# Linear attention's numerator with the sequence on the partitions: many short matmuls and transposes in place of few long ones

## The chip, the cores and the metric

The kernel runs on one core of one Trainium2 chip. A core has a matrix engine (TensorE, PE in the profile, with its weight loads listed apart as PEld), a vector engine (DVE), a scalar engine (ACT), GpSimd (POOL), and DMA queues that SyncE (SP) starts. Matmul results land in PSUM, in tiles of one bank each; this kernel's PSUM pool has 8 such tiles and every PSUM tile comes from it. DVE and ACT carry results from PSUM to SBUF. The kernel is written in a tile framework that works out the semaphores, gives out the buffers and may move an instruction against its neighbours.

The metric is the device time of one execution in microseconds, the median of several runs.

## The reference

Two linear attention blocks A and B with their own weights read the same input `x` (2048 rows, 640 columns, 32 heads of 20 columns). A gate mixes their outputs row by row.

```python
def _A_ref(x, wqkv, wo):                    # _B_ref is the same with B's weights
    H = 32; Dh = D // H                     # D = 640, Dh = 20, S = 2048
    q, k, v = ...(x @ wqkv)...              # each (B, H, S, Dh)
    phi = lambda t: jnp.where(t > 0, t + 1, jnp.exp(t)) + 1e-6
    pq, pk = phi(q), phi(k)
    kv = jnp.einsum("bhsd,bhse->bhde", pk, v)
    z = jnp.einsum("bhsd->bhd", pk)
    num = jnp.einsum("bhqd,bhde->bhqe", pq, kv)
    den = jnp.einsum("bhqd,bhd->bhq", pq, z)[..., None] + 1e-6
    o = num / den
    return o.transpose(...).reshape(B, S, D) @ wo

g = sigmoid((x * gate_w).sum(-1, keepdims=True))
out = g * A(x) + (1 - g) * B(x)
```

## The kernel before

The kernel keeps `x` transposed (`xT`, columns of `x` on the partitions, S = 2048 along the free side). In the constants, `P` is 128, `NCH` 512, `NS` = 4 blocks of 512 rows, `NQ` = 4 chunks of 128 rows in a block, `ST` = 16 chunks in all, and `DT` = `QT` = 5 tiles of 128 columns.

`q_group` makes 128 columns of phi(q) for 512 rows, transposed: 5 matmuls of 512 columns, two ACT activations, one DVE instruction that writes `pqT`. `kv_chunk` makes phi(k) and v for 128 rows with the rows on the partitions, in three PSUM tiles: 15 matmuls, two `ke` activations and two `vaug` copies on ACT, two `kr` instructions and one `pk` on DVE.

```python
def kv_chunk(blk, i, with_gate):
    # ... p0: 512 wide, p1: 448 wide, p2: 320 wide; 5 matmuls each
    nc.scalar.activation(out=e[:, 0:K0_W], in_=p0[:, 0:K0_W], func=ACT.Exp)          # ke
    nc.scalar.activation(out=e[:, K0_W:D], in_=p1[:, 0:K1_W], func=ACT.Exp)          # ke
    nc.vector.tensor_scalar(r[:, 0:K0_W], p0[:, 0:K0_W], 0.0, 1e-6, ...)             # kr
    nc.vector.tensor_scalar(r[:, K0_W:D], p1[:, 0:K1_W], 0.0, 1e-6, ...)             # kr
    nc.vector.scalar_tensor_tensor(out=pk[:, i, :], in0=e[:], in1=r[:], ...)         # pk
    nc.scalar.copy(out=vaug[...], in_=p1[...])      # first 16 heads of v
    nc.scalar.copy(out=vaug[...], in_=p2[...])      # last 16 heads of v
```

`phase_kvwin` then sums phi(k) times v over all rows. It leaves `KVbd`, a 640 by 640 matrix that holds the 20 by 20 block of each head on its diagonal and zeros elsewhere, and `Zsel`, with which `den_group` makes the 32 denominators of 128 rows, the rows on the partitions. `rec_ops` takes the reciprocals and multiplies them by the gate into `recs`, 32 values for each row.

The part that the change replaces is the numerator and its scaling. The result has to be `oT`, transposed, since `final_group` uses it as the stationary operand:

```python
def transposes(self, n):                       # of RecState
    pr = ps_tile_bf16(f"recT_{self.blk}")
    for q in range(NQ):
        i = n * NQ + q
        nc.tensor.transpose(out=pr[:H, q * P:(q + 1) * P], in_=self.recs[:, i, :], identity=identb[:])
    nc.vector.tensor_copy(out=self.recT[:H, n * NCH:(n + 1) * NCH], in_=pr[:H, :NCH])

def num_group(blk, oT, recT, j, n):
    dch = echunks[j]                           # the 2 or 3 tiles of pqT whose heads reach into tile j
    pn = ps_tile(f"num_{blk}")
    pr = ps_tile(f"rt_{blk}")
    for kk, c in enumerate(dch):
        nc.tensor.matmul(
            pn[:, :NCH], lhsT=KVbd[:, c, j * P:(j + 1) * P], rhs=pqT[:, c, n * NCH:(n + 1) * NCH],
            start=(kk == 0), stop=(kk == len(dch) - 1),
        )
    nc.tensor.matmul(                          # spreads 32 reciprocals over the 20 columns of each head
        pr[:, :NCH], lhsT=E[:, j * P:(j + 1) * P], rhs=recT[:, n * NCH:(n + 1) * NCH],
        start=True, stop=True,
    )
    numsb = work.tile([P, NCH], BF16, tag="numsb", name="numsb")
    nc.scalar.copy(out=numsb[:], in_=pn[:, :NCH])
    nc.vector.tensor_tensor(
        out=oT[:, j, n * NCH:(n + 1) * NCH], in0=numsb[:], in1=pr[:, :NCH], op=ALU.mult,
    )
```

`echunks` has 2, 3, 3, 3 and 2 tiles for the five values of j, 13 in all, so a block of the reference takes 4 x 13 = 52 `num` matmuls and 4 x 5 = 20 `rt` matmuls, each 512 columns wide, and 16 transposes of `recs`.

`final_group(i)` multiplies 128 rows of `oTA` and `oTB` by the two output matrices: 20 matmuls of 320 columns into two PSUM tiles, one copied out by ACT and one by DVE, then one DMA to the output.

The order in the program, from the denominators of A on:

```python
for i in range(LEAD_KV):                 # 4
    kv_chunk("B", i, False)
for n in range(NS):
    recA.transposes(n)
for n in range(NS):
    for j in range(QT):
        num_group("A", oTA, recTA, j, n)         # 20 groups in a row
# ... kv_chunk B 4 to 15, with q_group B of blocks 0 to 2 laid between them
phase_kvwin("B", ZselB)
# ... den_group B 0 to 11 and their rec_ops
for m in range(QT):
    q_group("B", m, NS - 1)
for n in range(NS - 1):
    recB.transposes(n)
# ... num_group B of block 0; den_group B 12 to 15 and their rec_ops
for n in range(NS):
    # ... for n > 0: num_group B of block n, 5 groups
    for q in range(NQ):
        final_group(n * NQ + q)
```

Of the kernel before, what the change touches and what calls it, by code (L numbers as in the profile page):

```python
# [8 lines left out]
P = 128  # L9
FP32 = mybir.dt.float32  # L10
BF16 = mybir.dt.bfloat16
ACT = mybir.ActivationFunctionType
ALU = mybir.AluOpType
# [3 lines left out]
def kernel(  # L17
# [11 lines left out]
    nc = tc.nc  # L29
# [3 lines left out]
    S, D = x2.shape  # L33
    H = 32
    Dh = D // H
    assert D % H == 0 and D % P == 0 and S % P == 0
    DT = D // P
    ST = S // P
    NCH = min(512, S)
    assert S % NCH == 0 and NCH % P == 0  # L40
    NS = S // NCH
    NQ = NCH // P
    QT = D // P
# [19 lines left out]
    for c in range(DT):  # L63
        h_lo = (c * P) // Dh
        h_hi = ((c + 1) * P - 1) // Dh
# [7 lines left out]
    echunks = []  # L73
# [7 lines left out]
    persist = ctx.enter_context(tc.tile_pool(name="persist", bufs=1))  # L81
    consts = ctx.enter_context(tc.tile_pool(name="consts", bufs=1))
    work = ctx.enter_context(tc.tile_pool(name="work", bufs=2))
    psum = ctx.enter_context(tc.tile_pool(name="psum", bufs=8, space=bass.MemoryType.PSUM))

    def ps_tile_bf16(name):
        return psum.tile([P, 2 * NCH], BF16, tag="ps", name=name)

    def ps_tile(name):
        return ps_tile_bf16(name).bitcast(FP32)  # L90
# [5 lines left out]
    pqT = persist.tile([P, QT, S], BF16, name="pqT")  # L96
    pk = persist.tile([P, ST, D], BF16, name="pk")
    vaug = persist.tile([P, ST, VAUG_W], BF16, name="vaug")
    oTA = persist.tile([P, QT, S], BF16, name="oTA")
    oTB = persist.tile([P, QT, S], BF16, name="oTB")  # L100
    KVbd = persist.tile([P, DT, D], BF16, name="KVbd")
    ZselA = persist.tile([P, DT, H], BF16, name="ZselA")
    ZselB = persist.tile([P, DT, H], BF16, name="ZselB")
    recTA = persist.tile([P, S], BF16, name="recTA")
    recTB = persist.tile([P, S], BF16, name="recTB")
    recsA = persist.tile([P, ST, H], BF16, name="recsA")
    recsB = persist.tile([P, ST, H], BF16, name="recsB")

    identb = consts.tile([P, P], BF16, name="identb")
    make_identity(nc, identb[:])  # L110
    E = consts.tile([P, D], BF16, name="E")
# [3 lines left out]
        out=E[:H], in_=E[:H], pattern=[[1, D]], compare_op=ALU.is_ge, fill=0.0, base=0,  # L115
# [3 lines left out]
        out=E[:H], in_=E[:H], pattern=[[-1, D]], compare_op=ALU.is_ge, fill=0.0, base=Dh - 1,  # L119
        channel_multiplier=Dh,  # L120
    )
    nc.vector.memset(recTA[:], 0.0)
    nc.vector.memset(recTB[:], 0.0)
    nc.gpsimd.memset(  # L124
        vaug[:].rearrange("p i (h t) -> p i h t", t=Dh + 1)[:, :, :, Dh:Dh + 1], 1.0
    )
# [4 lines left out]
    gcol = consts.tile([P, ST], FP32, name="gcol")  # L131
    gcolB = consts.tile([P, ST], FP32, name="gcolB")
# [72 lines left out]
    def kv_chunk(blk, i, with_gate: bool):  # L205
        nB = K1_W + V0_W
        nC = V1_W + (1 if with_gate else 0)
        sl = slice(i * P, (i + 1) * P)
        p0 = ps_tile(f"p0_{blk}")
        p1 = ps_tile(f"p1_{blk}")  # L210
        p2 = ps_tile(f"p2_{blk}")
        regions = [(p0, K0_W, OFF_K0), (p1, nB, OFF_K1), (p2, nC, OFF_V1)]
        for pt, w, off in regions:
            for c in range(DT):
                first, last = (c == 0), (c == DT - 1)
                nc.tensor.matmul(pt[:, :w], lhsT=xT[:, c, sl], rhs=Wr[:, c, off:off + w], start=first, stop=last)  # L216
        e = work.tile([P, D], BF16, tag="ke", name="ke")
        r = work.tile([P, D], BF16, tag="kr", name="kr")
        nc.scalar.activation(out=e[:, 0:K0_W], in_=p0[:, 0:K0_W], func=ACT.Exp)  # L219
        nc.scalar.activation(out=e[:, K0_W:D], in_=p1[:, 0:K1_W], func=ACT.Exp)  # L220
        nc.vector.tensor_scalar(r[:, 0:K0_W], p0[:, 0:K0_W], 0.0, 1e-6, op0=ALU.max, op1=ALU.add)
        nc.vector.tensor_scalar(r[:, K0_W:D], p1[:, 0:K1_W], 0.0, 1e-6, op0=ALU.max, op1=ALU.add)
        nc.vector.scalar_tensor_tensor(  # L223
            out=pk[:, i, :], in0=e[:], scalar=1.0, in1=r[:], op0=ALU.min, op1=ALU.add,
        )
        nc.scalar.copy(
            out=vaug[:, i, 0:VSPLIT_H * (Dh + 1)].rearrange("p (h t) -> p h t", t=Dh + 1)[:, :, 0:Dh],
            in_=p1[:, K1_W:K1_W + V0_W].rearrange("p (h t) -> p h t", t=Dh),
        )
        nc.scalar.copy(  # L230
            out=vaug[:, i, VSPLIT_H * (Dh + 1):VAUG_W].rearrange("p (h t) -> p h t", t=Dh + 1)[:, :, 0:Dh],
            in_=p2[:, 0:V1_W].rearrange("p (h t) -> p h t", t=Dh),
        )
        if with_gate:
            nc.scalar.activation(out=gexp[:, i:i + 1], in_=p2[:, nC - 1:nC], func=ACT.Exp, scale=-1.0)
# [31 lines left out]

    class RecState:

        def __init__(self, blk, Zsel, gc, recs, recT):  # L270
            self.blk = blk
            self.Zsel = Zsel
            self.gc = gc
            self.recs = recs
            self.recT = recT
            self.den_tiles = [ps_tile(f"den{n}_{blk}") for n in range(NS)]

        def den_group(self, i):
# [16 lines left out]
                op=ALU.mult,  # L295
            )

        def transposes(self, n):
            pr = ps_tile_bf16(f"recT_{self.blk}")
            for q in range(NQ):  # L300
                i = n * NQ + q
                nc.tensor.transpose(out=pr[:H, q * P:(q + 1) * P], in_=self.recs[:, i, :], identity=identb[:])
            nc.vector.tensor_copy(out=self.recT[:H, n * NCH:(n + 1) * NCH], in_=pr[:H, :NCH])

    def num_group(blk, oT, recT, j, n):
        dch = echunks[j]
        pn = ps_tile(f"num_{blk}")
        pr = ps_tile(f"rt_{blk}")
        for kk, c in enumerate(dch):
            nc.tensor.matmul(  # L310
                pn[:, :NCH], lhsT=KVbd[:, c, j * P:(j + 1) * P], rhs=pqT[:, c, n * NCH:(n + 1) * NCH],
                start=(kk == 0), stop=(kk == len(dch) - 1),
            )
        nc.tensor.matmul(  # L314
            pr[:, :NCH], lhsT=E[:, j * P:(j + 1) * P], rhs=recT[:, n * NCH:(n + 1) * NCH],
            start=True, stop=True,
        )
        numsb = work.tile([P, NCH], BF16, tag="numsb", name="numsb")
        nc.scalar.copy(out=numsb[:], in_=pn[:, :NCH])  # L319
        nc.vector.tensor_tensor(  # L320
            out=oT[:, j, n * NCH:(n + 1) * NCH], in0=numsb[:], in1=pr[:, :NCH], op=ALU.mult,
        )

    FH = D // 2

    def final_group(i):
        sl = slice(i * P, (i + 1) * P)
        o0 = ps_tile("o0")
        o1 = ps_tile("o1")
        steps = [(oTA, woA, j) for j in range(QT)] + [(oTB, woB, j) for j in range(QT)]  # L330
        for kk, (oT, wo, j) in enumerate(steps):
            first, last = (kk == 0), (kk == len(steps) - 1)
            nc.tensor.matmul(o0[:, :FH], lhsT=oT[:, j, sl], rhs=wo[:, j, 0:FH], start=first, stop=last)  # L333
            nc.tensor.matmul(o1[:, :FH], lhsT=oT[:, j, sl], rhs=wo[:, j, FH:D], start=first, stop=last)  # L334
        osb = work.tile([P, D], BF16, tag="osb", name="osb")
        nc.scalar.copy(out=osb[:, 0:FH], in_=o0[:, :FH])  # L336
        nc.vector.tensor_copy(out=osb[:, FH:D], in_=o1[:, :FH])  # L337
        nc.sync.dma_start(out=out2[sl, :], in_=osb[:])
# [21 lines left out]
            kv_chunk("A", arg, True)  # L360
    phase_gate()
    phase_kvwin("A", ZselA)
    recA = RecState("A", ZselA, gcol, recsA, recTA)
    for i in range(ST):
        recA.den_group(i)
    for n in range(NS):
# [1 line left out]
    load_w(B_wqkv, False, kv_first=True)  # L368

    LEAD_KV = min(ST, 4)  # L370
    for i in range(LEAD_KV):
        kv_chunk("B", i, False)
    for n in range(NS):
        recA.transposes(n)
    for n in range(NS):
        for j in range(QT):
            num_group("A", oTA, recTA, j, n)
    q_items_B = [("q", (n, m)) for n in range(NS - 1) for m in range(QT)]
    kv_items_B = [("kv", i) for i in range(LEAD_KV, ST)]
    for kind, arg in interleave(kv_items_B, q_items_B):  # L380
        if kind == "q":
            q_group("B", arg[1], arg[0])
        else:
            kv_chunk("B", arg, False)
    phase_kvwin("B", ZselB)
    recB = RecState("B", ZselB, gcolB, recsB, recTB)
    for i in range((NS - 1) * NQ):
        recB.den_group(i)
    for n in range(NS - 1):
        recB.rec_ops(n)  # L390
    for m in range(QT):
        q_group("B", m, NS - 1)
    for n in range(NS - 1):
        recB.transposes(n)
    if NS > 1:
        for j in range(QT):
            num_group("B", oTB, recTB, j, 0)
    for i in range((NS - 1) * NQ, ST):
        recB.den_group(i)
    recB.rec_ops(NS - 1)  # L400
    for n in range(NS):
        if n == NS - 1:
            recB.transposes(n)
        if n > 0 or NS == 1:
            for j in range(QT):
                num_group("B", oTB, recTB, j, n)
        for q in range(NQ):
            final_group(n * NQ + q)


# [28 lines left out]
```

## Time and profile before

| what | value |
|---|---|
| median time, 4 runs | 241.47 us (240.92 to 241.95) |
| span of the profiled execution | 239.1 us, 3821 instructions |
| matmuls | 1490 in the records, 225.4 us busy |
| DVE, ACT busy | 137.2 us, 127.7 us |
| moved by DMA | 12.05 MB |

The span starts with GpSimd and DMA work; the first matmul begins 8.9 us in. Block A's q, k and v take the time to 78.7 us. From 96.8 to 113.3 us stands block A's numerator, and from 113.3 to 162.0 us the rest of block B's k, v and q. From 174.4 us on, block B's numerator and the final groups take turns until the end.

A busy matmul engine in such a table means that matmuls are in flight, not how many; how close together they start is read from the chain of waits, where a run of matmuls on the path is given with its length and count.

### The profile page before, as it was taken

Reading aid. Unit: us, or ns where it says so; the run is one execution under the profiler, and the core shown is the slowest. Engines: PE = TensorE matmul, PEld = TensorE weight load, DVE = VectorE, ACT = ScalarE, POOL = GpSimd, SP = SyncE. Lnnn points to the kernel's source line nnn. Section 1 sums busy time; section 2 is a strip of 40 time slices with the busy share of each in tenths; the row PEclk is TensorE's granted clock in tenths of the full one; section 3 lists DMA queues with packets and bytes.
Section 4 is the critical chain, followed back from the end, with each engine's and each line's share of the span. In section 5 each row is a group of like instructions: output and inputs, shape, how many; then the busy total and the mean of one; then the engine's idle time right before and its main releaser. Section 6 shows DMA issues by size and latency. Waiting matters only on the chain.

```text
span 239.1 us, 3821 instructions
## 1 busy us (share of the span) xinstructions
PE 225.4 (94%) x1490; PEld 129.4 (54%) x1511; DVE 137.2 (57%) x256; ACT 127.7 (53%) x281; POOL 8.0 (3%) x12
## 2 busy tenths in 40 slices
PE   0599999999999999999999999999999999999994
PEld 0235555455545965544555555459547657576572
DVE  3456656575657487898665656564884252432511
ACT  2057677867776326677668677763581241421410
POOL 8400000000000000000000000000000000000000
PEclk9999999999999999999999999999999999999999
DMA  7999800000001910000000000000000101101011
GB/s 192 189 272 190 285 0 1 1 3 0 0 0 14 358 45 0 3 0 1 0 4 0 0 0 3 0 0 3 0 4 27 55 30 55 55 30 55 27 56 58
DMA packets 18787, 12.05 MB, mean 50 GB/s; under 512 B 11601, under 2 KB 18769, under 8 KB 18769
## 3 DMA queue, kind: packets, MB, share of 16 engines
q1 hardware_dynamic: 18768, 11.80, 18.2%
q8 instruction: 12, 0.20, 0.4%
q14 instruction: 7, 0.05, 0.1%
HBM read 6.55 MB, written 2.62 MB: 38 GB/s over the span
## 4 chain that ended last, share of the span: by engine, by line
PE 94%; POOL 3%; DVE 1%; issue 1%; POOLq 0%; DVEq 0%
PE p_A L216 18%; PE p_B L216 18%; PE pq_A L190 10%; PE o L334 9%; PE o L333 9%; PE pq_B L190 9%; PE num_A L310 5%; PE num_B L310 4%; PE rt_B L314 2%; PE rt_A L314 2%; PE kva_B L249 1%; PE kva_A L249 1%; PE pb L184 1%; POOL KVbd L127 1%; POOL vaug L124 1%; PE kvb_B L249 1%
## 5 line engine op out<-in xcount | busy, mean ns | idle before, releaser
L216 PEld LDWEIGHTS <-xT 128*128 128x128 bf16 x480 | 46.7, 97 | 43.5
L200 DVE SCALAR_TENSOR_TENSOR pqT<-qe,qr 128x512 bf16<-128x512 bf16 x40 | 27.6, 690 | 40.4 <-ACT qr L199 40.4
L216 PE MATMUL p_A<-Wr,xT 128*128 128x512 bf16 (+2 forms) x238 | 45.3, 344 | 0.1
L216 PE MATMUL p_B<-Wr,xT 128*128 128x448 bf16 (+2 forms) x236 | 45.1, 343 | 0.2
L190 PEld LDWEIGHTS <-Wr 128*128 128x128 bf16 x200 | 19.8, 100 | 20.9 <-issue 2.7
L223 DVE SCALAR_TENSOR_TENSOR pk<-ke,kr 128x640 bf16<-128x640 bf16 x32 | 26.4, 825 | 1.1
L337 DVE CAST osb<-o 128x320 bf16<-128x320 f32 x16 | 7.9, 492 | 32.7 <-PE o L334 30.1
L336 ACT CAST osb<-o 128x320 bf16<-128x320 f32 x16 | 6.8, 426 | 37.0 <-PE o L333 37.0
L190 PE MATMUL pq_A<-xT,Wr 128*128 128x512 bf16 x96 | 25.1, 398 | 0.2
L190 PE MATMUL pq_B<-xT,Wr 128*128 128x512 bf16 x95 | 23.4, 379 | 0.2
L333 PE MATMUL o<-woB,oTB 128*128 128x320 bf16 x80 | 22.2, 299 | 0.0
L334 PE MATMUL o<-woB,oTB 128*128 128x320 bf16 x80 | 22.2, 299 | 0.0
L334 PE MATMUL o<-woA,oTA 128*128 128x320 bf16 x80 | 22.2, 299 | 0.0
L333 PE MATMUL o<-woA,oTA 128*128 128x320 bf16 x80 | 22.2, 299 | 0.0
L198 ACT ACTIVATE qe<-pq_A 128x512 bf16<-128x512 f32 x20 | 11.9, 597 | 16.5 <-PE pq_A L190 16.5
L198 ACT ACTIVATE qe<-pq_B 128x512 bf16<-128x512 f32 x20 | 11.9, 598 | 11.5 <-PE pq_B L190 11.5
L310 PEld LDWEIGHTS <-KVbd 128*128 128x128 bf16 x104 | 9.9, 98 | 11.3
L320 DVE TENSOR_TENSOR oTB<-numsb,rt_B 128x512 bf16<-128x512 bf16 x20 | 13.5, 686 | 3.8 <-ACT numsb L319 3.1
L320 DVE TENSOR_TENSOR oTA<-numsb,rt_A 128x512 bf16<-128x512 bf16 x20 | 13.6, 688 | 2.0 <-ACT numsb L319 0.9
L219 ACT ACTIVATE ke<-p_B 128x512 bf16<-128x512 f32 x16 | 9.6, 597 | 9.1 <-PE p_B L216 9.1
L319 ACT CAST numsb<-num_B 128x512 bf16<-128x512 f32 x20 | 11.7, 586 | 4.8 <-PE num_B L310 3.8
L319 ACT CAST numsb<-num_A 128x512 bf16<-128x512 f32 x20 | 11.7, 586 | 4.5 <-PE num_A L310 3.0
(73 smaller groups left out, 258.7 us busy)
## 6 DMA issues: line engine op xcount, KB each, us to landing
out_dram<-osb SPq DMA_DIRECT2D x16, 160.0 KB, 1.8
Wr<-in_A_wqkv_dram SPq DMA_DIRECT2D x3, 800.0 KB, 6.5
Wr<-in_B_wqkv_dram SPq DMA_DIRECT2D x3, 800.0 KB, 6.7
woA<-in_A_wo_dram SPq DMA_DIRECT2D x1, 800.0 KB, 5.7
woB<-in_B_wo_dram SPq DMA_DIRECT2D x1, 800.0 KB, 7.2
xT<-in_A_x_dram SPq DMA_TRANSPOSE x10, 4.2
Wr<-in_gate_w_dram SPq DMA_DIRECT2D x1, 1.2 KB, 8.0
```

The costliest lines, as they stand in the source:

```text
L190: nc.tensor.matmul(pq_ps[:, :NCH], lhsT=Wr[:, c, OFF_Q + m * P:OFF_Q + (m + 1) * P], rhs=xT[:, c, n * NCH:(n + 1) * NCH], start=(c == 0), ...
L198: nc.scalar.activation(out=e[:], in_=pq_ps[:, :NCH], func=ACT.Exp)
L200: nc.vector.scalar_tensor_tensor(out=pqT[:, m, n * NCH:(n + 1) * NCH], in0=e[:], scalar=1.0, in1=r[:], op0=ALU.min, op1=ALU.add,)
L216: nc.tensor.matmul(pt[:, :w], lhsT=xT[:, c, sl], rhs=Wr[:, c, off:off + w], start=first, stop=last)
L219: nc.scalar.activation(out=e[:, 0:K0_W], in_=p0[:, 0:K0_W], func=ACT.Exp)
L223: nc.vector.scalar_tensor_tensor(out=pk[:, i, :], in0=e[:], scalar=1.0, in1=r[:], op0=ALU.min, op1=ALU.add,)
L310: nc.tensor.matmul(pn[:, :NCH], lhsT=KVbd[:, c, j * P:(j + 1) * P], rhs=pqT[:, c, n * NCH:(n + 1) * NCH], start=(kk == 0), stop=(kk == len ...
L314: nc.tensor.matmul(pr[:, :NCH], lhsT=E[:, j * P:(j + 1) * P], rhs=recT[:, n * NCH:(n + 1) * NCH], start=True, stop=True,)
L319: nc.scalar.copy(out=numsb[:], in_=pn[:, :NCH])
L320: nc.vector.tensor_tensor(out=oT[:, j, n * NCH:(n + 1) * NCH], in0=numsb[:], in1=pr[:, :NCH], op=ALU.mult,)
L333: nc.tensor.matmul(o0[:, :FH], lhsT=oT[:, j, sl], rhs=wo[:, j, 0:FH], start=first, stop=last)
L334: nc.tensor.matmul(o1[:, :FH], lhsT=oT[:, j, sl], rhs=wo[:, j, FH:D], start=first, stop=last)
```

## The change

The numerator is turned round. Instead of `KVbd` as the stationary operand with 512 rows streamed past it, 128 rows of `pqT` are stationary and the columns of `KVbd` stream past, and only those columns that are not zero. The result `o` then has the rows on the partitions, where `recs` already has its 32 values for each row. So DVE can scale straight out of PSUM with a broadcast along the 20 columns of a head, and the matmul that spread the reciprocals, the transposes of `recs` and the ACT copy `numsb` go. The price is that `o` has to be transposed afterwards: 5 times 4 transposes for each block of 512 rows, and 5 ACT copies of their results into `oT`.

The program's order changes too. Block A's chunks are no longer one stretch of their own but lie between the k and v chunks 2 to 10 of block B. Block B's first four chunks lie between the last q groups, and the others between the final groups, one block of 512 rows ahead.

```diff
-    recTA = persist.tile([P, S], BF16, name="recTA")
-    recTB = persist.tile([P, S], BF16, name="recTB")
...
-    nc.vector.memset(recTA[:], 0.0)
-    nc.vector.memset(recTB[:], 0.0)
...
-        def transposes(self, n): ...          # and all of num_group
+    FH = (H // 2) * Dh                        # 320, one half of the heads to each PSUM tile
+    o_pieces = []                             # [tile of pqT, first column, end column, PSUM tile, start, stop]
...                                            # widths for each 128 rows: 140, 20, 120, 20, 60 | 80, 20, 120, 20, 120
+    def o_chunk(blk, i, recs, oN):
+        q = i % NQ
+        po = [ps_tile(f"o0_{blk}"), ps_tile(f"o1_{blk}")]
+        lhsT = pqT[:, :, i * P:(i + 1) * P]
+        for (c, u, v, bank, st, sp) in o_pieces:
+            base = 0 if bank == 0 else FH
+            nc.tensor.matmul(
+                po[bank][:, u - base:v - base], lhsT=lhsT[:, c], rhs=KVbd[:, c, u:v], start=st, stop=sp,
+            )
+        nh0 = FH // Dh
+        nc.vector.tensor_tensor(
+            out=oN[:, q, 0:FH].rearrange("p (h t) -> p h t", t=Dh),
+            in0=po[0][:, 0:FH].rearrange("p (h t) -> p h t", t=Dh),
+            in1=recs[:, i, 0:nh0, None].to_broadcast([P, nh0, Dh]),
+            op=ALU.mult,
+        )
...                                            # the same for po[1] and the other 16 heads
+    def o_transposes(blk, n, oN, oT, use_scalar_copy=True):
+        for j in range(QT):
+            pt = ps_tile_bf16(f"oT_{blk}")
+            for q in range(NQ):
+                nc.tensor.transpose(
+                    out=pt[:, q * P:(q + 1) * P], in_=oN[:, q, j * P:(j + 1) * P], identity=identb[:],
+                )
+            if use_scalar_copy:
+                nc.scalar.copy(out=oT[:, j, n * NCH:(n + 1) * NCH], in_=pt[:, :NCH])
...
+    def kv_and_o(i):
+        kv_chunk("B", i, False)
+        n, half = divmod(i - 2, 2)
+        if half == 0 and 0 < n <= NS:
+            o_transposes("A", n - 1, pend[n - 1], oTA)
+        if 0 <= n < NS:
+            if half == 0:
+                pend[n] = new_oN()
+            for q in (2 * half, 2 * half + 1):
+                o_chunk("A", n * NQ + q, recsA, pend[n])
...                                            # kv_and_o takes the place of kv_chunk in block B
+    oN = new_oN()
     for m in range(QT):
         q_group("B", m, NS - 1)
-    for n in range(NS - 1):
-        recB.transposes(n)
-    if NS > 1:
-        for j in range(QT):
-            num_group("B", oTB, recTB, j, 0)
+        if m < NQ:
+            o_chunk("B", m, recsB, oN)
     for i in range((NS - 1) * NQ, ST):
         recB.den_group(i)
     recB.rec_ops(NS - 1)
+    o_transposes("B", 0, oN, oTB)
     for n in range(NS):
-        if n == NS - 1:
-            recB.transposes(n)
-        if n > 0 or NS == 1:
-            for j in range(QT):
-                num_group("B", oTB, recTB, j, n)
+        more = n + 1 < NS
+        if more:
+            oN = new_oN()
         for q in range(NQ):
+            if more:
+                o_chunk("B", (n + 1) * NQ + q, recsB, oN)
             final_group(n * NQ + q)
+        if more:
+            o_transposes("B", n + 1, oN, oTB)
```

More of the change, by code (lines that the diff above doesn't have):

```diff
@@ L268, with __init__ @@
     class RecState:
-        def __init__(self, blk, Zsel, gc, recs, recT):
+        def __init__(self, blk, Zsel, gc, recs):
             self.blk = blk
@@ L274, in __init__ @@
             self.recs = recs
-            self.recT = recT
             self.den_tiles = [ps_tile(f"den{n}_{blk}") for n in range(NS)]
@@ L296, in rec_ops @@
             )
-        def transposes(self, n):
-            pr = ps_tile_bf16(f"recT_{self.blk}")
-            for q in range(NQ):
[L301 to L322, printed above, removed]
@@ L324 @@
-    FH = D // 2
+    FH = (H // 2) * Dh
+    assert FH % Dh == 0
+    o_pieces = []
+    prev_hi = 0
+    bank_started = [False, False]
+    for c in range(DT):
+        h_lo = (c * P) // Dh
+        h_hi = ((c + 1) * P - 1) // Dh
+        lo, hi = h_lo * Dh, (h_hi + 1) * Dh
+        ranges = []
+        if prev_hi > lo:
+            ranges.append((lo, min(hi, prev_hi)))
+        if hi > prev_hi:
+            ranges.append((max(lo, prev_hi), hi))
+        for (a, b) in ranges:
+            for (u, v) in ((a, min(b, FH)), (max(a, FH), b)):
+                if u < v:
+                    bank = 0 if u < FH else 1
+                    o_pieces.append([c, u, v, bank, not bank_started[bank], False])
+                    bank_started[bank] = True
+        prev_hi = hi
@@ new lines @@
+    assert prev_hi == D
+    for bank in range(2):
+        idxs = [k for k, pc in enumerate(o_pieces) if pc[3] == bank]
+        o_pieces[idxs[-1]][5] = True
+    def o_chunk(blk, i, recs, oN):
[14 more added lines that the diff above has]
+        )
+        nc.vector.tensor_tensor(
+            out=oN[:, q, FH:D].rearrange("p (h t) -> p h t", t=Dh),
+            in0=po[1][:, 0:D - FH].rearrange("p (h t) -> p h t", t=Dh),
+            in1=recs[:, i, nh0:H, None].to_broadcast([P, H - nh0, Dh]),
+            op=ALU.mult,
+        )
@@ new lines, in o_transposes @@
+    def o_transposes(blk, n, oN, oT, use_scalar_copy=True):
+        for j in range(QT):
+            pt = ps_tile_bf16(f"oT_{blk}")
+            for q in range(NQ):
+                nc.tensor.transpose(
+                    out=pt[:, q * P:(q + 1) * P], in_=oN[:, q, j * P:(j + 1) * P], identity=identb[:],
+                )
+            if use_scalar_copy:
+                nc.scalar.copy(out=oT[:, j, n * NCH:(n + 1) * NCH], in_=pt[:, :NCH])
+            else:
+                nc.vector.tensor_copy(out=oT[:, j, n * NCH:(n + 1) * NCH], in_=pt[:, :NCH])
@@ L326, in final_group, with new_oN, o_block @@
+    def new_oN():
+        return work.tile([P, NQ, D], BF16, tag="oN", name="oN")
+    def o_block(blk, n, recs, oT):
+        oN = work.tile([P, NQ, D], BF16, tag="oN", name="oN")
+        for q in range(NQ):
+            o_chunk(blk, n * NQ + q, recs, oN)
+        o_transposes(blk, n, oN, oT)
     def final_group(i):
@@ L362 @@
     phase_kvwin("A", ZselA)
-    recA = RecState("A", ZselA, gcol, recsA, recTA)
+    recA = RecState("A", ZselA, gcol, recsA)
     for i in range(ST):
@@ L370 @@
     LEAD_KV = min(ST, 4)
-    for i in range(LEAD_KV):
[L372 to L375, printed above, removed]
-        for j in range(QT):
-            num_group("A", oTA, recTA, j, n)
+    pend = {}
+    def kv_and_o(i):
[8 more added lines that the diff above has]
+                o_chunk("A", n * NQ + q, recsA, pend[n])
+    for i in range(LEAD_KV):
+        kv_and_o(i)
     q_items_B = [("q", (n, m)) for n in range(NS - 1) for m in range(QT)]
@@ L383 @@
         else:
-            kv_chunk("B", arg, False)
+            kv_and_o(arg)
     phase_kvwin("B", ZselB)
-    recB = RecState("B", ZselB, gcolB, recsB, recTB)
+    recB = RecState("B", ZselB, gcolB, recsB)
     for i in range((NS - 1) * NQ):
@@ L400 @@
     recB.rec_ops(NS - 1)
+    o_transposes("B", 0, oN, oTB)
     for n in range(NS):
-        if n == NS - 1:
-            recB.transposes(n)
-        if n > 0 or NS == 1:
-            for j in range(QT):
-                num_group("B", oTB, recTB, j, n)
+        more = n + 1 < NS
+        if more:
+            oN = new_oN()
         for q in range(NQ):
+            if more:
+                o_chunk("B", (n + 1) * NQ + q, recsB, oN)
             final_group(n * NQ + q)
+        if more:
+            o_transposes("B", n + 1, oN, oTB)
 _INS = ['A_x', 'A_wqkv', 'A_wo', 'B_x', 'B_wqkv', 'B_wo', 'gate_w']
```

## The prediction

> **What bounds the kernel now.** I read the page's busy times and slices first, then the chain of waits in order of time (start us, us, what), then the groups by line with their shapes, then stretches of the span.
>
> From the page of the kernel before:
>
> ```profile
> PE 225.4 (94%) x1490; PEld 129.4 (54%) x1511; DVE 137.2 (57%) x256; ACT 127.7 (53%) x281; POOL 8.0 (3%) x12
> ...
> PEclk9999999999999999999999999999999999999999
> ...
> PE 94%; POOL 3%; DVE 1%; issue 1%; POOLq 0%; DVEq 0%
> ```
>
> The reader is to see that TensorE is both the busiest engine and the chain that sets the end, at full clock throughout, and that DVE and ACT have over 40% of the span free. Time taken from TensorE's stream comes off the end, unless DVE or ACT then becomes late. Busy matmuls overlap, so the price of one must be read from how close together they start. The chain gives runs of matmuls that follow one another without a wait:
>
> ```profile
> 81.93 2.09 PE kvb_A L249 x32
> ...
> 84.69 1.75 PE den_A L281 x64
> ...
> 96.85 1.00 PE recT_A L302 x16
> 98.60 0.65 PE num_A L310 x3
> ```
>
> Length by count gives the pitch: 65.3 ns for 147 columns, 27.3 ns for 32 columns, 62.5 ns for a 128-column transpose, 216.7 ns for 512 columns. Between 147 and 512 columns that is (216.7 - 65.3) / 365 = 0.415 ns a column and 4.3 ns fixed. At 32 columns this line would give 17.6 ns, and 27.3 was measured: a floor, set by something other than the columns. Each of these matmuls has its own weight load, so the pitches contain it.
>
> The side engines, from the groups by shape (busy us, mean ns of one, idle before):
>
> ```profile
> L319 ACT CAST numsb<-num_A 128x512 bf16<-128x512 f32 x20 | 11.7, 586 | 4.5 <-PE num_A L310 3.0 <-PE recT_A L302 0.8 <-DVE oTA L320 0.5
> L320 DVE TENSOR_TENSOR oTA<-numsb,rt_A 128x512 bf16<-128x512 bf16 x20 | 13.6, 688 | 2.0 <-ACT numsb L319 0.9 <-PE num_A L310 0.5
> L337 DVE CAST osb<-o 128x320 bf16<-128x320 f32 x16 | 7.9, 492 | 32.7 <-PE o L334 30.1 <-ACT osb L336 2.6
> L261 DVE TENSOR_TENSOR KVbd<-kva_A,BD 128x140 bf16<-128x140 f32 x2 | 0.6, 298 | 0.0
> ```
>
> Last, stretches of the span (length, then busy us and count of PE, PEld, DVE, ACT and POOL): A's numerator, the rest of B's k, v and q, and the start of B's numerator.
>
> ```profile
> 97.00:113.50 16.50, 16.39 (x87) 7.84 (x87) 14.49 (x24) 11.95 (x22) 0.00 (x0) 1.00 0.01 1
> 113.50:162.20 48.70, 48.44 (x253) 24.94 (x257) 29.80 (x51) 34.78 (x77) 0.00 (x0) 1.00 0.00 1
> ...
> 169.80:179.00 9.20, 9.13 (x50) 4.32 (x51) 8.18 (x16) 7.70 (x14) 0.00 (x0) 1.00 0.01 3
> ```
>
> TensorE has almost no gap in any of them, also where DVE is busy for 14.5 of 16.5 us. So today neither evacuation nor PSUM holds it up.
>
> **What the Trainium skill says.** "TensorE: Matmul & The Clock Gate", section "Back-to-back issue gap", puts the warm gap at N / 2.4 + 2.5 ns, 215.8 ns for 512 columns; the trace agrees (216.7). The section "Wait — 56ns, not 53.3ns?" of that page says that the start-to-start time of small matmuls never drops below about 25 ns; 27.3 ns in `den_A` agrees, and is what a 20-column piece will cost. Part 4 of the page, "PE-mode transpose", gives about 275 ns for a transpose in one kernel; in a stream this trace has 62.5 ns from one to the next, so I use that. "PSUM — Partial Sum Buffer" says in "Terms" that two engines must not access one bank at once. In the trace ACT's `vaug` copy waits 11.6 us in all for DVE's `kr` on the same tile, so in the crowded stretch DVE and ACT delay each other.
>
> **The change part by part, on TensorE.** Removed: `num`, 52 for each of A and B, and `rt`, 20 for each, makes 144 matmuls at 216.7 ns = 31.2 us; 32 transposes of `recs` at 62.5 ns = 2.0 us. Together 33.2 us. The trace agrees: A's numerator reaches from 97.8 to 113.3 us, 15.5 us, and 72 x 216.7 ns = 15.6.
>
> Added, for 128 rows: ten matmuls. Four of 20 columns at the floor, 4 x 27.3 = 109; three of 120 columns at 54.1 = 162; one of 140 at 62.4; one of 80 at 37.5; one of 60 at 29.2. Sum 400 ns. For 32 chunks 12.8 us. Transposes: 2 x 4 x 5 x 4 = 160 at 62.5 ns = 10.0 us. Together 22.8 us. Though the matmuls grow in number by 480 - 176 = 304, the stream gets shorter by 33.2 - 22.8 = 10.4 us. The reason is columns: 2,304 `num` and `rt` columns for each 128 rows before, of which most are zeros of `KVbd` or copies of a reciprocal; 720 and 640 after.
>
> **On DVE and ACT.** DVE loses 40 instructions of about 687 ns, 27.5 us, and eight copies of `recT`, 3.2 us at about 400. It gains 64 of 128x320 out of PSUM in fp32. The `KVbd` row gives 298 ns for 140 columns in the same 20-wide groups, and the cast of 320 columns took 492, so I take 490 each: 31.4 us. ACT loses 40 copies of 586 ns and gains 40 copies of the same size, which I put at the same 586. Their totals hardly move; what moves is when they run. A's share leaves a stretch where it had 16.5 us to itself and goes among chunks 2 to 10 of B.
>
> The stretch of chunks 4 to 9: for a chunk DVE had 29.80 / 12 = 2.5 us and ACT 34.78 / 12 = 2.9 us. Each chunk now brings two `o_chunk`, 4 x 0.49 = 2.0 us of DVE, and on average 2.5 copies, 1.5 us of ACT. That makes 4.5 us DVE and 4.4 us ACT. TensorE has 48.7 / 12 = 4.06 us, plus 2 x 0.40, plus 10 transposes, 0.63: 5.5 us. On average TensorE stays the slowest. But the copies come five in a row in every second chunk: ACT then has 2.9 + 2.9 = 5.8 us plus the 0.4 us that it waits for `kr` on the shared tile, against 2.7 + 1.25 + 0.80 + 1.08 = 5.8 us of TensorE. With 8 PSUM tiles, of which such a chunk takes 13, TensorE can't run far ahead. I choose 1 us of stalls for the whole stretch.
>
> The start of B's numerator: TensorE makes q group, chunk, q group, chunk, to the fifth q group: 5 x 1.08 + 4 x 0.40 = 7.0 us from 169.2 on, to 176.2. On DVE the reciprocals and the first `pqT` end at 172.5 in the trace. Behind them stand, in the order of the compiled program, eight `oN` and three `pqT` before the last `oN` that the transposes need. Instructions on DVE start closer together than their durations (`pqT` at 118.44, `kr` at 119.05, with 690 ns each: 0.61 us), so I take 0.42 for an `oN` and 0.62 for a `pqT`: 3.4 + 1.9 = 5.3, to 177.8. TensorE waits 1.6 us. Before, it had a full `num` block to do there.
>
> Among the final groups a chunk stands one final group, 2.7 us, ahead of its transposes, and the five copies, 2.9 us after one `osb` copy of 0.43, are hidden by the chunk and by A's half of the next final group; B's half needs the last of them 1.25 + 0.40 + 1.36 + 1.08 = 4.1 us after the transposes began. The two memsets gone from the start lay beside the 8 us of GpSimd that the first matmul waits for, and give nothing. The tail after the last matmul is unchanged.
>
> Sum: -33.2 + 22.8 + 1.0 + 1.6 = -7.8 us; 241.5 - 7.8 = 233.7. I predict 233.5.
>
> **The rivals.** (1) The side engines become the bound in the mixed stretch. For it: averages within 1.1 us of TensorE's, bursts that equal it, `pqT` waiting for ACT and `vaug` for DVE in fixed order, three of a chunk's tiles held until both are done. Against it: pitches on DVE and ACT are shorter than durations, and the chunks from 11 on are light. If each of six chunks cost 1 us, the stalls would be 6 instead of 1: about 238.5. (2) Short matmuls cost more than the floor, because weight load and matmul of 20 columns can't overlap as with 32, or since a transpose of 128 weight columns is slower than one of 32: at 40 ns for the 128 short ones and 80 ns for a transpose 1.6 + 2.8 us more: about 238. For it: only that these shapes aren't in the trace. Against it: `den_A` loads a full 128x128 weight for each matmul at 27.3 ns. (3) No stalls at all, as before, and 57 ns a transpose: 241.5 - 11.3 = 230.2. Nothing in the profile makes the added work dearer than the work removed, so a slower kernel needs (1) and (2) at their worst together.
>
> **Range and chances.** The low end is rival 3, the high end rival 1 or 2 alone. 2% faster is 236.6, which leaves 2.9 us over the 233.5 for stalls that I mis-sized. I give 0.78 to faster, 0.18 to within 2%, 0.04 to slower.
>
> **What would show it.** Runs of `o_A` should have about 40 ns a matmul, transposes 55 to 63; TensorE's busy time should fall by some 8 us or more; `oN` should take about 490 ns, a copy of `oT` 586. Gaps of TensorE in the mixed stretch of over 3 us in all, released by ACT or DVE, mean rival 1; a gap well over 2 us before `oT_B` means that I mis-sized the start of B. Pitches over 70 ns for `oT` or over 50 for `o` mean rival 2.

## The result and the profile after

The changed kernel takes 229.58 us (median of 10 runs, 229.15 to 230.54), before 241.3 us (median of 16). The ratio is 0.952, interval 0.950 to 0.954: 11.7 us less, where the prediction had 8.0 and a range that ended at its rival 3, 230.2 by its sum. The direction and the main cause, a shorter stream of TensorE, are as predicted; the gain is half as large again.

From the page of the changed kernel, the busy times and the chain by engine:

```profile
PE 215.0 (94%) x1796; PEld 135.6 (59%) x1815; DVE 131.5 (58%) x270; ACT 123.4 (54%) x281; POOL 8.0 (4%) x12
...
PE 90%; DVE 4%; POOL 3%; ACT 1%; issue 1%; POOLq 0%; DVEq 0%
```

The reader is to see 306 more matmuls in the records and 10.4 us less busy time of TensorE, which still is the chain. DVE's 4% are new: a stretch of the chain at the start of B's numerator now runs through it.

The chain in order of time (start us, us, what) gives the prices of the new pieces, in the stretch where A's numerator lies among B's k and v chunks:

```profile
98.74 0.77 PE o_A L325 x20
99.51 2.71 PE p_B L212 x15
102.22 1.12 PE oT_A L346 x20
103.33 0.76 PE o_A L325 x20
104.10 0.30 PE pq_B L186
104.45 0.81 PE pq_B L186 x3
105.26 2.71 PE p_B L212 x15
```

Two chunks take 0.77 us, so one takes 0.385; 20 transposes take 1.12 us, 56 ns each. Nothing stands between these pieces: TensorE goes from chunk to k and v and to transposes without a gap. The next piece is a q group, and it is 0.08 us late: its five matmuls take from 104.10 to 105.26, 1.16 us, where another q group of this chain takes 1.08. The same happens behind each of the three bursts of transposes that have chunks behind them (0.08 to 0.09 us, 0.26 in all).

The groups by shape (busy us, mean ns of one, idle before) and the mixed stretch (length, then busy us and count of PE, PEld, DVE, ACT and POOL) show the side engines:

```profile
L350 ACT COPY oTA<-oT_A 128x512 bf16<-128x512 bf16 x20 | 10.3, 628 | 0.0
L329 DVE TENSOR_TENSOR oN<-o_A,recsA 128x320 bf16<-128x320 f32 x16 | 7.7, 484 | 1.5 <-PE o_A L325 1.5
```

```profile
95.20:134.20 39.00, 38.73 (x374) 24.74 (x377) 31.12 (x64) 27.59 (x61) 0.00 (x0) 1.00 0.01 2
```

`oN` takes the 0.49 us that was predicted, the copies somewhat more than the predicted 586 ns, and yet TensorE is busy for 38.73 of 39.00 us. The view of the waits lists two of TensorE in the whole span, of which the first stood there before too. The records of neighbouring matmuls overlap, and a gap shorter than the overlap, like the 0.08 us above, doesn't appear in it.

```profile
PE pm L175 <- POOL E L116: 8.7, 1, 8.7
PE oT_B L346 <- ACT qr L195: 0.3, 1, 0.3
```

### The profile page after: what moved, and what is told of

The parts are those of the page before. It is cut to its first block, busy times and chain, and to the rows that moved or that the text cites. A ratio compares the mean times of both kernels' runs of the same rounds, so it can differ in the third digit from the quotient of the medians.

```text
span 228.7 us, 4389 instructions
## 1 busy us (share of the span) xinstructions
PE 215.0 (94%) x1796; PEld 135.6 (59%) x1815; DVE 131.5 (58%) x270; ACT 123.4 (54%) x281; POOL 8.0 (4%) x12
## 4 chain that ended last, share of the span: by engine, by line
PE 90%; DVE 4%; POOL 3%; ACT 1%; issue 1%; POOLq 0%; DVEq 0%
PE p_A L212 19%; PE p_B L212 19%; PE pq_A L186 11%; PE o L370 10%; PE o L371 10%; PE pq_B L186 7%; PE o_A L325 3%; PE oT_A L346 2%; PE o_B L325 2%; PE oT_B L346 2%; PE kva_A L245 1%; PE kva_B L245 1%; PE pb L180 1%; DVE rcp L285 1%; POOL KVbd L123 1%; POOL vaug L120 1%
## 5 line engine op out<-in xcount | busy, mean ns | idle before, releaser
L212 PE MATMUL p_B<-Wr,xT 128*128 128x320 bf16 (+2 forms) x235 | 45.2, 343 | 0.2
L186 PE MATMUL pq_A<-xT,Wr 128*128 128x512 bf16 x96 | 26.2, 412 | 0.2
L186 PE MATMUL pq_B<-xT,Wr 128*128 128x512 bf16 x92 | 23.9, 378 | 0.4
L325 PEld LDWEIGHTS <-pqT 128*128 128x128 bf16 x320 | 14.9, 96 | 2.0
L215 ACT ACTIVATE ke<-p_B 128x512 bf16<-128x512 f32 x16 | 9.7, 603 | 10.4 <-PE p_B L212 10.3
L217 DVE TENSOR_SCALAR kr<-p_A 128x512 bf16<-128x512 f32 x16 | 11.0, 687 | 3.9 <-ACT ke L215 3.9
L195 ACT ACTIVATE qr<-pq_B 128x512 bf16<-128x512 f32 x20 | 12.0, 599 | 0.0
L195 ACT ACTIVATE qr<-pq_A 128x512 bf16<-128x512 f32 x20 | 11.8, 592 | 0.0
L217 DVE TENSOR_SCALAR kr<-p_B 128x512 bf16<-128x512 f32 x16 | 11.0, 687 | 0.8 <-ACT ke L215 0.6
```

The source lines that it names most:

```text
L186: nc.tensor.matmul(pq_ps[:, :NCH], lhsT=Wr[:, c, OFF_Q + m * P:OFF_Q + (m + 1) * P], rhs=xT[:, c, n * NCH:(n + 1) * NCH], start=(c == 0), ...
L195: nc.scalar.activation(out=r[:], in_=pq_ps[:, :NCH], func=ACT.Relu)
L325: nc.tensor.matmul(po[bank][:, u - base:v - base], lhsT=lhsT[:, c], rhs=KVbd[:, c, u:v], start=st, stop=sp,)
```

## Where the 11.7 us come from

The start of the sums over phi(k) and v (`kva_A`, then `kva_B`) cuts the span into three parts in every run. This table has their lengths from the timelines, in us.

| kernel | up to `kva_A` | `kva_A` to `kva_B` | `kva_B` to the end |
|---|---|---|---|
| before | 78.5 | 83.5 | 77.1 |
| changed | 79.6 | 77.7 | 71.3 |

The first part is the same program in both but for two memsets. Its length differs with its first 25 matmuls of q, here before and changed:

```profile
11.92 7.16 PE pq_A L190 x25
11.93 8.27 PE pq_A L186 x25
```

The 1.1 us between them is the whole difference. In the trace a part of these matmuls start 0.43 us apart instead of 0.216, though the page shows the granted clock as full there. How many do so isn't set by the kernel: a run below with the same program up to `kva_A` as the changed kernel takes 6.93 us for the 25. Why is not shown here. The parts behind are therefore the better measure; the intervals of the ratios of whole times reach 0.4 to 0.7 us to each side.

The other two parts each lose 5.7 to 5.8 us. From TensorE's stream alone each should lose what one block loses. Before, 72 `num` and `rt` matmuls at 0.216 and 16 transposes of `recs` at 0.056 are 16.45 us; 16 chunks at 0.385 and 80 transposes at 0.056 are 10.64 us; the difference is 5.81. So the gaps that came and those that went nearly cancel, in the mixed stretch to less than 0.1 us and in the last part to 0.1 us.

The count by pitches also says where the shorter stream comes from. In both blocks together, `num` took 104 x 0.216 = 22.5 us, and its replacement, chunks with transposes, takes 12.3 + 9.0 = 21.3 us. The other 10.4 us are the 40 `rt` matmuls (8.6) and the 32 transposes of `recs` (1.8), which nothing replaces on TensorE. So turning the product round gains 1.2 us by itself; most of the gain is that the reciprocals need no spreading when the rows are on the partitions. This is a count; no run takes the two apart.

## The experiments

The theory: the gain is the shorter stream of TensorE, and it comes through whole because DVE and ACT keep up. The rivals: the new order itself hides something; and DVE, ACT or the PSUM tiles are close to taking over.

**The order without the new maths.** A's 20 `num` groups of the kernel before are laid among B's k and v chunks 2 to 9.

```diff
-    for n in range(NS):
-        for j in range(QT):
-            num_group("A", oTA, recTA, j, n)
+    def kv_and_num(i):
+        kv_chunk("B", i, False)
+        if i == 2: ...                            # the transposes of recs
+        if 2 <= i < 10:
+            for n, j in numA[(20 * (i - 2)) // 8:(20 * (i - 1)) // 8]:
+                num_group("A", oTA, recTA, j, n)
```

> The numerator of before (long matmuls, reciprocals spread by a matmul), but A's 20 groups laid among B's k and v chunks 2 to 9 as in the changed kernel. Theory (the gain is the shorter TensorE stream alone): TensorE had no gap in A's stretch of before, so laying it elsewhere gives nothing: 241.3, within 0.7 us. Rival (part of the gain is the interleaving, which hides the DVE and ACT work of A): 3 us or more of the 11.7 appear here, 238 or less.

Measured: 241.16 us, ratio 1.000 (0.999 to 1.002). From `kva_A` to `kva_B` it takes 83.5 us, as before. The order of A's half alone gives nothing: TensorE had next to no gaps to fill there (busy for 16.39 of 16.50 us before). B's half of the order was not run with the old maths.

**The new maths without the order.** All chunks of A stand behind B's fourth k and v chunk.

```diff
-        n, half = divmod(i - 2, 2)
-        ...                                       # two chunks behind each of B's chunks 2 to 9
+        if i == LEAD_KV - 1:
+            for n in range(NS):
+                pend[n] = new_oN()
+                for q in range(NQ):
+                    o_chunk("A", n * NQ + q, recsA, pend[n])
+                    if q == 1 and n > 0:
+                        o_transposes("A", n - 1, pend[n - 1], oTA)
+            o_transposes("A", NS - 1, pend[NS - 1], oTA)
```

> The short matmuls and transposes of the changed kernel, but all 16 chunks of A in one stretch after B's fourth k and v chunk, where before had its numerator; B's half as in the changed kernel. In that stretch TensorE needs 16 x 0.383 + 80 x 0.056 = 10.6 us, DVE 32 oN starts 0.40 us apart = 12.8 us. Theory (the side engines are hidden only because the work is spread): DVE sets the stretch and TensorE gets 2 to 3 us of gaps, released by DVE: 231.5 to 232.5. Rival (the order does not matter at all): 229.6, within 0.5.

Measured: 232.84 us, ratio 0.966 (0.964 to 0.969), 3.3 us over the changed kernel, 0.3 more than the expected range. The part from `kva_A` to `kva_B` is 81.1 us, 3.4 more. The chain of this run, in A's stretch:

```profile
98.47 0.40 DVE oN L329
98.88 0.40 DVE oN L335
...
101.32 0.24 PE oT_A L346
101.59 0.59 ACT oTA L350
102.22 0.38 PE oT_A L346 x4
102.61 1.93 PE o_A L325 x40
```

The chain runs through DVE and ACT where before it ran through TensorE alone. So A's half of the order is worth nothing for the old maths and 3.3 us for the new: left in one stretch, the short matmuls outrun their evacuation (the instructions of DVE and ACT that carry their results out of PSUM).

**Six PSUM tiles in place of eight.** `bufs=8` becomes `bufs=6` in the PSUM pool of the changed kernel.

> The changed kernel with 6 PSUM tiles instead of 8. Theory (DVE and ACT follow close behind TensorE, so PSUM has room to spare in the mixed stretch): 1 us or less more than 229.6. Rival (my first one from the prediction: PSUM tiles come free just in time, and depth is what saves it): 4 us or more, with gaps of TensorE among chunks 4 to 9 of B, released by ACT or DVE.

Measured: 233.74 us, ratio 0.969 (0.966 to 0.972): 4.2 us more, the amount that the rival named, but only half of it in the stretch that the rival meant. In the profiles 2.0 us lie between `kva_A` and `kva_B`, 1.2 after and 0.4 before; the rest is between these profiles and the medians. The same place in the timelines of the changed kernel and of this one (start, length, what), the chunks behind a burst of transposes:

```profile
103.17 0.93 PE L325 MATMUL o_A<-KVbd,pqT 128*128 128x140 bf16 x20
```

```profile
103.54 1.70 PE L325 MATMUL o_A<-KVbd,pqT 128*128 128x140 bf16 x20
```

The 20 matmuls behind a burst of transposes take 1.70 us instead of 0.93, and so they do behind all three bursts of A that have chunks behind them; elsewhere they take 0.93. Three times 0.77, less the 0.26 us that the q groups behind waited already with eight tiles, are the 2.0 us. The transposes have taken five tiles that ACT empties only after its `vaug` copies. With eight tiles the chunks find room; with six they wait. My theory expected 1 us at most and falls here: the room is there, but it isn't large. What the 1.2 us of B's half wait for stays open.

**Without the 20-column matmuls.** This leaves out, for four heads of each half, the part of the sum that lies in the neighbouring tile, only to weigh the short matmuls.

```diff
-                if u < v:
+                if u < v and v - u != Dh:
```

> The changed kernel without the four 20-column matmuls of each chunk; this leaves out the part of a head that lies in the neighbouring tile of pqT, so four heads get part of their sum only. 128 matmuls are gone. Theory (floor of 27.3 ns for a short matmul with its weight load, as in den): 128 x 27.3 = 3.5 us less, 226.1. Rival (the columns count, 20 x 0.415 + 4.3 = 12.6 ns): 1.6 us less, 228.0.

Measured: 228.06 us, ratio 0.945 (0.942 to 0.947), 1.5 us less than the changed kernel. By the time alone the rival would have it, but the chain of this run says otherwise:

```profile
101.80 0.43 ACT vaug L222
102.23 0.33 ACT vaug L226
102.56 0.98 ACT oTA L350 x2
103.58 1.24 PE pq_B L186 x5
104.82 2.71 PE p_B L212 x15
107.53 0.56 PE o_A L325 x12
```

Two chunks take 0.56 us instead of 0.77, so a 20-column matmul costs (0.77 - 0.56) / 8 = 26 ns: the floor. TensorE got 128 x 26 ns = 3.3 us shorter, and a part of it was lost again: 1.5 us came through by the medians, 2.4 by the two parts behind `kva_A` of the profiles, 1.0 of 1.7 in the first of them. There the q group behind the chunks waits for a tile of `oT` that ACT has to copy; it starts 0.29 us behind them, three times, where it was 0.08 late in the changed kernel. So this wait is already there in the changed kernel, if small, and what is taken from TensorE's stream in front of it turns in part into waiting.

**More work for DVE, and more for ACT.** Both are built on the changed kernel. One does the first of A's two `oN` instructions of each chunk twice, the other each of A's copies of `oT`; both write the same values again.

```diff
-        nc.vector.tensor_tensor(out=oN[:, q, 0:FH]..., in0=po[0]..., ...)
+        for _ in range(2 if blk == "A" else 1):
+            nc.vector.tensor_tensor(out=oN[:, q, 0:FH]..., in0=po[0]..., ...)
```

> The changed kernel, with the first of A's two oN instructions of each chunk done twice (the same values written again): 16 more on DVE, 0.40 us apart, 6.4 us, all among B's chunks 2 to 9, where DVE was busy 31.1 of 39.0 us. Theory (the stretch has just enough room: six PSUM tiles and the missing short matmuls both showed new gaps): 1 to 3 us slower than the changed kernel, 230.6 to 232.6. Rival (DVE has 7.9 us free there and they can be used): within 0.5 us of 229.6.

```diff
-                nc.scalar.copy(out=oT[:, j, n * NCH:(n + 1) * NCH], in_=pt[:, :NCH])
+                for _ in range(2 if blk == "A" else 1):
+                    nc.scalar.copy(out=oT[:, j, n * NCH:(n + 1) * NCH], in_=pt[:, :NCH])
```

> The changed kernel, with each of A's 20 copies of oT done twice on ACT: 20 more, 0.51 us apart, 10.2 us, in bursts of ten among B's chunks 4 to 10, where ACT was busy 27.6 of 39.0 us. Theory (just enough room, and the copies hold five PSUM tiles for twice as long): 2 to 4 us slower than the changed kernel, 231.6 to 233.6. Rival (ACT has 11.4 us free there): within 0.5 us of 229.6.

Measured with more DVE work: 229.94 us, ratio 0.953 (0.951 to 0.956), not to be told from the changed kernel. With more ACT work: 231.62 us, ratio 0.960 (0.957 to 0.962), 2.0 us more, 1.7 of it between `kva_A` and `kva_B`. The stretch with DVE's work, and then TensorE's timeline with ACT's:

```profile
94.00:132.00 38.00, 37.65 (x362) 23.87 (x365) 35.39 (x77) 27.18 (x60) 0.00 (x0) 1.00 0.01 2
```

```profile
101.78 1.28 PE L346 MATMUL oT_A<-identb,oN 128*128 128x128 bf16 x20
102.89 0.74 PE L325 MATMUL o_A<-KVbd,pqT 128*128 128x140 bf16 x15
104.23 0.35 PE L325 MATMUL o_A<-KVbd,pqT 128*128 128x80 bf16 x5 [0.60 <-ACT oTA L351]
```

DVE can be busy for 35.4 of 38.0 us with TensorE busy for all but 0.35 us, so for DVE my theory of a stretch at its edge falls. ACT, busy for less of its stretch (33.7 of 41.0 us), costs time, by the place where it holds PSUM: the last five matmuls of two chunks wait 0.60 us for a tile of the copies. The copies start 0.48 us apart and not 0.51 as I had put it, so ACT got 9.6 us of work more and DVE 6.4; most of both was hidden. Together with the six tiles this points to the burst of five tiles, and not to an engine's share, as what is near its limit.

**The denominator as a 21st column.** Built on the changed kernel, to beat it. `KVbd` gets the sum of phi(k) as a 21st column of each head, so the chunk's own matmuls make the denominators; the 160 `den` matmuls, `Zsel` and the eight large reciprocals go, and one chunk of A stands behind each of B's 16 k and v chunks.

```diff
-    KVbd = persist.tile([P, DT, D], BF16, name="KVbd")
+    KVbd = persist.tile([P, DT, H * (Dh + 1)], BF16, name="KVbd")
...                                               # in o_chunk, for each of the two PSUM tiles
-        nc.vector.tensor_tensor(out=oN[...], in0=po[...], in1=recs[...], op=ALU.mult)
+        nc.vector.reciprocal(out=rv, in_=pv[:, :, Dh])
+        nc.vector.scalar_tensor_tensor(
+            out=oN[...], in0=pv[:, :, 0:Dh], scalar=gc[:, i:i + 1],
+            in1=rv[:, :, None].to_broadcast([P, nh0, Dh]), op0=ALU.mult, op1=ALU.mult,
+        )
```

> Built on the changed kernel, to beat it: the denominator becomes a 21st column of each head in KVbd, so the 160 den matmuls and Zsel go, the ten matmuls of a chunk have 756 columns instead of 720, and DVE takes two reciprocals of 16 and two multiplications by gate and reciprocal for each chunk, in place of eight large reciprocals. A's chunks stand one behind each k and v chunk of B, 0 to 15. TensorE: 160 x 27.3 = 4.4 us less, 32 x 36 x 0.415 = 0.5 us more, so if its stream is still the bound, 225.7 (225.0 to 226.7). Rival (the 64 small reciprocals, some 0.25 us each, make DVE the bound and eat the gain): 228 or more.

Measured: 225.41 us, ratio to before 0.934 (0.932 to 0.937), faster than both kernels. The parts are 77.5, 75.9 and 69.6 us: each of the last two loses 1.7 to 1.9 against the changed kernel, 3.6 together where TensorE's sum had 3.9. The medians differ by 4.2; the rest is in the first part, where the matmuls that made a mask for `Zsel` went too (TensorE's first wait, for GpSimd, is 5.9 us there and not 8.7), and which varies in any case. DVE's busy time rose from 131.5 to 134.9 us, since the eight large reciprocals that went (7.2 us) were less than what came, above all

```profile
L304 DVE RECIPROCAL rcp<-o_A 128x16 f32<-128x16 f32 x32 | 6.1, 228 | 1.5 <-PE o_A L296 1.5
```

and as much for B. That was hidden, as the doubled `oN` had been.

## Why the prediction was right in kind and too small

- **TensorE is the bound before and after: right.** A's half of the order alone gave nothing, and both parts of the span lose what the stream loses.
- **Removed, 33.2 us:** 2 x 16.45 = 32.9 us. Right.
- **Added, 22.8 us: mis-sized.** 32 x 0.385 + 160 x 0.056 = 21.3 us. The floor for 20 columns held (26 ns, 27.3 assumed). Too dear by 1.5 us, 1.0 of it the transposes: 62.5 ns came from 16 transposes, 1.00 us up to the first `num`, and this holds 0.1 us of gap. Before, too, they start 56 ns apart: all 16 take 1.07 us in the timeline, the last one lasts 0.22, and 0.85 / 15 is 57 ns.
- **"I choose 1 us of stalls for the whole stretch": failed.** The three gaps of 0.08 to 0.09 us are all that came, 0.26 us, and 0.19 us of before went (0.09 in front of and 0.10 behind the transposes of `recs`). I had set ACT's burst against TensorE's with durations on one side, 5 x 586 ns = 2.9 us, and start-to-start distances on the other. In the trace the five copies take 2.56 us with the end of the last, which makes (2.56 - 0.63) / 4 = 0.48 us from one to the next, though one lasts 628 ns:

```profile
102.88 2.56 ACT L350 COPY oTA<-oT_A 128x512 bf16<-128x512 bf16 x5
103.56 0.49 DVE L329 TENSOR_TENSOR oN<-o_A,recsA 128x320 bf16<-128x320 f32 x1 [0.50 <-PE o_A L325]
103.97 0.48 DVE L335 TENSOR_TENSOR oN<-o_A,recsA 128x320 bf16<-128x320 f32 x1
...
107.33 0.28 ACT L216 ACTIVATE ke<-p_B 128x128 bf16<-128x128 f32 x1 [0.29 <-PE p_B L212]
```

  In the chunk that follows the burst, ACT has caught up: its second `ke` waits 0.29 us for TensorE. From `vaug` at 102.24 to the next `vaug` at 107.99 it has 5.1 us of its own to do, by starts, and waits for the rest of the 5.75, where I had reckoned with 6.2 against 5.8. `oN` starts 0.40 us after `oN` with 0.48 to 0.49 us each. The mechanism of rival 1 is real, as six tiles and doubled copies showed, but this kernel stands only at its beginning.
- **"TensorE waits 1.6 us" at the start of B's numerator: failed in size.** I took it that the transposes have to wait for the last `oN`. In the compiled program twelve of the twenty come ahead of it, and eight later:

```profile
171.30 0.83 PE L346 MATMUL oT_B<-identb,oN 128*128 128x128 bf16 x12
172.35 0.48 DVE L335 TENSOR_TENSOR oN<-o_B,recsB 128x320 bf16<-128x320 f32 x1
172.56 0.44 PE L346 MATMUL oT_B<-identb,oN 128*128 128x128 bf16 x5 [0.28 <-ACT qr L195]
```

  The twelve are done at 172.13, before the last `oN` starts at 172.35, so they can only be of the first three chunks. And the next one is released by `qr` of ACT, 0.28 us, not by `oN`. From 164.73 us to the first final matmul at 173.62, 8.89 us, TensorE had 23 q matmuls, five chunks, 20 transposes and four `den` to do, 8.1 us by their distances: 0.8 us of gaps. Against them stand gaps of before that went and that I had not counted. At one place TensorE waited for `recT` to be copied back:

```profile
221.11 0.39 PE L314 MATMUL rt_B<-recTB,E 128*128 128x512 bf16 x1 [0.31 <-DVE recTB L303]
```

  By the starts this gap is 0.26 us, and in front of and behind each of the two bursts of transposes of `recs`, at 174.44 and 220.09 us, stand another 0.09 and 0.10. Together they are 0.64 us, so that 0.15 us is left of the 0.8; the last part asks for 0.1.
- **The sum.** The gaps that came are 0.26 + 0.8 us, those that went 0.19 + 0.64, so 0.2 us net where I had 2.6. -32.9 + 21.3 + 0.2 = -11.4 us; the two parts of the profiles lose 11.5, and the medians 11.7. Of the 3.9 us between 7.8 and 11.7, 2.4 are the stalls and 1.5 the pitches; what was removed was 0.3 less than I had, and the other 0.3 lie between this sum and the medians.
- **The range** was wrong by its own text: rival 3, no stalls and 57 ns a transpose, is nearly what happened, and I had put the low end on it, as if nothing could lie beyond. Rival 2 is out (38.5 ns a matmul of `o`, 56 a transpose); rival 1 is out for eight tiles, with 0.26 us of gaps where its sign was over 3.

The Trainium skill, "VectorE: DVE Perf Modes", section "The DRAIN you can't avoid", says that the next instruction doesn't start until the pipe is empty, and adds that one that is not held starts earlier. The rows of `oN` above are of the second kind: the next `oN` starts 0.08 us before the last one's end, so durations of DVE must not be added up either.

## What to carry to other kernels

Ask which layout lets a factor for each row be applied without spreading it first. Here that was worth more than the product itself: for 512 rows, 18 matmuls of 512 columns and 4 transposes of `recs`, 4.1 us, gave way to 40 short matmuls and 20 transposes, 2.7 us. A block-diagonal matrix can leave out its zero columns as the moving operand, which it could not as the stationary one here; most of that gain (22.5 us against 12.3) went into transposing the result back (9.0 us). Where the bound engine's work gets shorter, put the side engines' work beside other matmuls and count PSUM tiles that a burst holds, not only shares of busy time. And when two engines are set against each other, use start-to-start distances for both.

## What the runs showed of the hardware

Transposes of 128x128 in bf16 follow one another every 56 ns. A matmul of 20 columns with its own weight load takes 26 ns of the stream, as much as 62 columns of a wide one at 0.415 ns. ACT copies of 512 columns that last 628 ns start 0.48 us apart, and DVE instructions of 0.48 us 0.40 us apart. Of the first 25 matmuls of 512 columns a part start 0.43 us apart instead of 0.216, so that the 25 took 7.16 us in one execution and 8.27 in another.
